# Left-over frequencies of the inverse feature transform stacked through HBM for tiles 6 to 15, and the sums of late tiles on GpSimd

## The chip, the cores and the metric

The kernel runs on one core of one Trainium2 chip. The metric is the device time of one execution in microseconds. Its engines are named as the profile names them: PE is TensorE, whose weight loads are PEld, DVE is VectorE, ACT is ScalarE, POOL is GpSimd, and SP is SyncE, which only issues transfers here. Each engine works through its own instructions in program order.

## What is computed

One block of a spectral network on 2048 tokens of 640 features, in float32: layer norm, a two-dimensional real Fourier transform over tokens and features, a filter, the inverse transform and a residual; then layer norm, a bilinear gated feed-forward of width 1728, and a residual.

```python
def _A_ref(x, w_r, w_i):
    X = rfft2(x, axes=(-2, -1))
    X = X * (w_r + 1j * w_i)
    return irfft2(X, s=(S, D), axes=(-2, -1))

def _B_ref(x, w_gate, w_up, w_down):
    h = einsum("bsd,df->bsf", x, w_gate) * einsum("bsd,df->bsf", x, w_up)
    return einsum("bsf,fd->bsd", h, w_down)

h = x + _A_ref(_layernorm(x), w_r, w_i)
h2 = h + _B_ref(_layernorm(h), w_gate, w_up, w_down)
```

## The kernel before, in words

The transform runs as products with tables of cosines and sines. Tokens are split in 16 tiles of 128 (`t`, 0 to 15). First comes the token transform of each tile (`s1_mm`), then, for 16 groups of token frequencies `g`, the feature transform (`d_mm`), the filter and the first half of the inverse token transform (`is2_mm`). Its result lies in `qm` (the 4 x 128 main feature frequencies, float32) and `qr` (64 left-over frequencies, 128 to 191, and frequency 192 in row 0; rows 0 to 63 hold the high part of each value, rows 64 to 127 the low part, both in float32r).

The stage that the change touches is the loop over `t` behind it. For each tile:

- `id_mm(t)`, the inverse feature transform, writes a pair of PSUM banks `eo`. Four float32 products of `qm` with the table `imt` (161 columns each; the profile counts each as two instructions) give even and odd halves of real and imaginary parts, and five float32r products of `qr` with the table `irt` (322 columns each) add the left-over frequencies. `irt` is part of the tile `xt`, whose second half is free until the transposes of tiles 4 to 7 write it.
- `unfold(t)`: ScalarE copies one half of `eo` to `s` (L650); VectorE forms sum and difference in `q` (L654, L655), then the first half of the output row, `yt` (L656); GpSimd forms the mirrored half (L658).
- `is1_mm(t)`, the last token transform, multiplies `yt` with the table `cit` into PSUM `y`; `acc(t)` (L671 with a running total for tiles 0 to 7, L669 for the rest) adds it to the residual `X[t]`.

The loop issues, for each `t`: the transposes of a normalised tile from `t` = 9 on (`turn_mm`, `y<-ident,zb` in the profile; `turn_hi` on ScalarE and `turn_lo`, L716, on VectorE), `unfold(t + 2)`, `id_mm(t + 3)`, side work on ScalarE (`aside`: squares for the layer norm L192, weight pieces L599, the normalisation L686), `is1_mm(t)`, `acc(t)`. `eo` has two pairs of banks, so `id_mm(t + 3)` waits until `unfold(t + 1)` has read its pair. The small scale operations of the layer norm (L188, L194, L202 to L205, L679, on 2 or 3 columns) are spread among VectorE's operations of `unfold` by `zipped`, which divides a list of side work evenly over the main operations.

The loads of three weight pieces (`raw0`) are issued on SP ahead of the loop. The next load on SP, `load_raw(0)` (L868), uses the space of `cit` and so waits for the last `is1_mm`. In the forward transform the same left-over work is stacked already for groups 5 to 14: `spread` writes rows of `s1r` to a scratch tensor in HBM (`sfar`), `stack` reads them back so that 99 rows hold high, low and high parts, and `d_mm` uses four passes for six.

```python
parts((ps[:, 0], ps[:, 1]), main,
      [(b, qr[:, k, t], irt[:, c]) for c, b, k in ((0, 0, 0), (2, 0, 0), (1, 1, 1), (3, 0, 1), (4, 1, 1))])
```

Of the kernel before, what the change touches and what calls it, by code (L numbers as in the profile page):

```python
# [25 lines left out]
RWHERE = ((1, 0), (0, 0), (1, 160), (0, 160))  # L26
RW = (160, 194, 162, 162)
PLAIN, LAST = 5, 15
AGAIN = {0: (5, 3), 1: (8, 2, "qt"), 5: (10, 3), 7: (13, 2, "qt")}
NR = 4  # L30
AHEAD = 5
# [8 lines left out]
def view(t, offset, dims):  # L40
    return bass.AP(tensor=t.tensor, offset=t.offset + offset, ap=[list(t.ap[0])] + [list(d) for d in dims])


def f32(ap):
    return ap.bitcast(F32)


def zipped(main, side):
    n = len(main)
    for i, f in enumerate(main):  # L50
        f()
        for h in side[i * len(side) // n:(i + 1) * len(side) // n]:
            h()
# [21 lines left out]
def tile_spectral_glu(ctx: ExitStack, tc: tile.TileContext, x, wf, wgu, wlast, wdown, wdlast,  # L75
                      cc, ci, fmain, frem, imain, irem, mm, out):
    nc = tc.nc
# [4 lines left out]
    far = ctx.enter_context(tc.tile_pool(name="far", bufs=1, space=bass.MemoryType.DRAM))  # L82
    ctx.enter_context(tc.manual_schedule())

    tt, act = nc.vector.tensor_tensor, nc.scalar.activation
# [28 lines left out]
    def mmx(o, l, r, start, stop):  # L114
        nc.tensor.matmul(o, l, r, start=start, stop=stop, skip_group_check=True)  # L115
# [13 lines left out]
    def home(tag, shape, name, dt=F32):  # L129
        return keep.tile(shape, dt, tag=tag, name=name)  # L130
# [142 lines left out]
    def s1_main(t, ps, a, b):  # L273
        act(view(s1, 4 * t + 2048 * a, [[2048, b - a], [64, 32], [1, 4]]),
            ps[:, a * P:b * P].rearrange("p (c g m) -> p c g m", c=b - a, g=32), AF.Copy)
# [18 lines left out]
    for ts, when, aside, root in GROUPS:  # L294
        k = len(when)
# [16 lines left out]
    for t in range(NT):  # L312
        if t == 1:
            nc.gpsimd.dma_start(frall, frem)
        if t >= 1:
# [18 lines left out]
            if t < AHEAD - 1:  # L334
                s1_rest(t - 1)
                main = lambda: s1_main(t - 1, PS1[t - 1][0], 0, 4)
# [55 lines left out]
    qr = home("qr", [P, 2, NT, P], "qr", F32R)  # L392
    PD, T, PU, Y, PI = {}, {}, {}, {}, {}

    def parts(ps, main, rest):
        for k, (b, o, w, l, r) in enumerate(main):
            mmx(ps[b][:, o:o + w], l, r, k < 2, False)
        for k, (b, l, r) in enumerate(rest):
            mmx(ps[b][:, 0:NQ], l, r, False, k >= len(rest) - 2)
# [21 lines left out]
    def stack(g, n, tag="dC"):  # L421
        o = home(tag, [P, 4, n, P], "st", F32R)
        src = sfar[:, :, :, g - PLAIN:g - PLAIN + n].rearrange("q l r g n -> q (l r) (g n)")
        for a, b, r in ((0, 66, 0), (66, 99, 0)):
            nc.sync.dma_start(f32(o[a:b].rearrange("p q g n -> p q (g n)")),
                              src[:, r:r + b - a].rearrange("q r n -> r q n"))
        for i in range(n):
            ST[g + i] = o[:, :, i]
# [9 lines left out]
    def s2_mm(g):  # L438
        if g >= NG - 2:
            ps = PU[g] = bank("re"), bank("im")  # L440
        else:
            PU[g] = pools["y"].tile([P, 2, 512], F32, tag="u", name="u", bufs=1)
            ps = PU[g][:, 0], PU[g][:, 1]
        for h in range(2):
            nc.tensor.matmul(ps[h][:, 0:NQ], WM[g][0][:, h], T[g][:, h], start=True, stop=True)  # L445
# [92 lines left out]
    for g in range(NG - 1):  # L538
        s2_mm(g)
        if g + 2 < NG:  # L540
            d_mm(g + 2)
        if g >= 5 and g in AGAIN:
            stack(*AGAIN[g])
        if g + 3 == NG:
            xt = home("big", [P, 2, 5, 2, 512], "xt", F32R)
            irt = xt[:, 1].rearrange("p k l n -> p (k l n)")[:, 0:5 * NQ].rearrange("p (c q) -> p c q", c=5)
        if g == NG - 2:
            nc.gpsimd.dma_start(irt, irem)
        if g == NG - 2:
            s2_mm(g + 1)  # L550
            filt_half(g, 0, True)
            is2_out(g - 2)
        if g >= 1:
            is2_mm(g - 1)
        if g < NG - 2:
            filt(g)
        else:
            late = [filt_half(g, 1), filt_half(g + 1, 0), filt_half(g + 1, 1, True)]
            for f in (late[0][0], late[1][0], late[1][1], late[2][1]):
                f()  # L560
        if g + 3 < NG:
            load_wm(g + 3)
        if g + 2 < NG:
            d_out(g + 2)
        if g >= 1:
            if g != NG - 3:
                is2_out(g - 1)
            if g + 2 < NG:
                load_wi(g + 2)
        if g < 2:  # L570
            stack(*AGAIN[g])
        elif g == 2:
            spread(PLAIN + 5, LAST)
        if g == 6:
            nc.sync.dma_start(cit, ci)
            nc.sync.dma_start(imt, imain)
# [26 lines left out]
    def load_direct(blk, raws, engine=nc.gpsimd):  # L603
        w = home("wA" if blk == 0 else "wB", [P, 3840], "wdir", F32R)
        return [split_in(NC - 1, cut(w, 0, 2, 640), wlast, raws[:1], engine),
                split_in(NC - 2, cut(w, 1280, 2, 1280), wgu[NC - 2], raws[1:], engine)]
# [29 lines left out]

    PE_, PY, YT, Z = {}, {}, {}, {}

    def id_mm(t):
        ps = PE_[t] = pair("eo")  # L640
        main = [(b, o, 161, qm[:, c, t], imt[:, c]) for c, (b, o) in enumerate(((0, 0), (1, 0), (0, 161), (1, 161)))]
        parts((ps[:, 0], ps[:, 1]), main,
              [(b, qr[:, k, t], irt[:, c]) for c, b, k in ((0, 0, 0), (2, 0, 0), (1, 1, 1), (3, 0, 1), (4, 1, 1))])

    def unfold(t, side, turns=()):
        ps = PE_[t]
        s = wk([P, 2, 161], "s")
        q = wk([P, 4, 161], "q")
        y = YT[t] = yt[:, t % 6]
        act(s, ps[:, :, 161:322], AF.Copy)  # L650
        for k in turns:
            turn_hi(k)
        zipped([
            lambda: tt(q[:, 0:2], ps[:, :, 0:161], s, op=OP.add),  # L654
            lambda: tt(q[:, 2:4], ps[:, :, 0:161], s, op=OP.subtract),  # L655
            lambda: tt(view(y, 0, [[320, 2], [1, 161]]), q[:, 0::2], q[:, 1::2], op=OP.add),  # L656
        ] + [lambda k=k: turn_lo(k) for k in turns], side)
        nc.gpsimd.tensor_tensor(view(y, 639, [[-320, 2], [-1, 159]]), q[:, 0::2, 1:160], q[:, 1::2, 1:160],  # L658
                                op=OP.subtract)

# [45 lines left out]
    def turn_hi(t):  # L706
        hi, pk = turned(t, 0)
        act(hi, pk, AF.Copy)
        if t == 0:
            TJ["b"] = home("dA", [P, 4, 4, P], "bt")  # L710
        if t < 4:
            act(TJ["b"][:, t], pk[:, 0:4], AF.Copy)

    def turn_lo(t):
        lo, pk = turned(t, 1)
        tt(lo, pk, f32(turned(t, 0)[0]), op=OP.subtract)  # L716
        if t % 8 >= 4:
            j = t % 4
            d = TJ[j] = wk([P, 4, P], "tj")
            b = TJ["b"][:, j]  # L720
            tt(d[:, 0:2], pk[:, 0:2], b[:, 0:2], op=OP.subtract)
            tt(d[:, 2:4], pk[:, 2:4], d[:, 0:2], op=OP.subtract)
# [62 lines left out]
    aside = [[] for _ in range(NT + 8)]  # L785
    dside = [[] for _ in range(NT + 8)]
    tside = [[] for _ in range(NT + 8)]
    scrap = xt[:, 1].rearrange("p k l n -> p (k l n)")[:, 2048:2048 + D]
    yt = home("wB", [P, 6, D], "yt")
    zb = home("dB", [P, 4, D], "zb")  # L790
    for ts in (range(3), range(3, 6), range(6, 8)):
        n, t0 = len(ts), ts[-1] + 1
# [11 lines left out]
    tside[NT - 1] = []  # L804
    raw0 = home("dA", [P, 3, D], "raw0")
    jobs = load_direct(0, [raw0[:, i] for i in range(3)])
    for i, (h, l) in enumerate((h, l) for hs, ls in jobs for h, l in zip(hs, ls)):
        aside[1 + i] += [h, l]
    id_mm(0)
# [274 lines left out]
    for n, (blk, p) in enumerate(steps):  # L1084
# [143 lines left out]
        for ci in range(2):  # L1228
            c = 2 * p + ci
            side = {n: [] for n in range(8)}  # L1230
# [41 lines left out]
            if blk == 0 and c in (6, 8):  # L1272
# [10 lines left out]
                for i in range(4):  # L1283
                    k = 4 * (c // 2 - 3) + i
# [10 lines left out]
def tables():  # L1295
# [19 lines left out]
    def rows(kind, ds):  # L1315
        r = np.zeros((len(ds), 2, NQ))
        for i, d in enumerate(ds):
# [3 lines left out]
            else:  # L1321
# [42 lines left out]
    def f4(a):  # L1364
        return np.ascontiguousarray(a, np.float32)

    def split(a):
        a = f4(a)
        hi = ((a.view(np.uint32) + np.uint32(0x800)) & np.uint32(0xFFFFF000)).view(np.float32)
        return f4(np.stack([hi, a - hi], 1))  # L1370

    inv = np.zeros((2, NF, 2, NQ))
    d = np.arange(161)
    for i, f in enumerate(fr):
        a = 1.0 if f in (0, 320) else 2.0
        o = slice(0, 161) if f % 2 == 0 else slice(161, 322)
# [54 lines left out]
```

## Time and profile before

| what | us |
|---|---|
| median of 3 runs | 687.5 (686.91 to 688.5) |
| profiled execution | 688.04 |
| its span, first to last instruction | 686.3 |
| granted TensorE clock over the span | 1.000 |
| the loop over tiles, first `eo` to the last load of weights behind it | 111.36 to 167.57 |
| VectorE's sums L656, 16 of them | 8.1 busy |
| GpSimd's sums L658, 16 of them | 16.2 busy |

The profiled execution is one run; its time is the span and what lies around it. A row of the timeline gives start and duration, engine, line, operation, output and inputs with their shapes. PE's matmuls overlap, so the step between two starts, not the duration, tells what one costs. "idle before" at a row's end is how long the engine stood still ahead of it, and what ended that.

### The profile page before, as it was taken

The numbers are of one execution on the slowest core, as the hardware profiler recorded it, in microseconds if no ns is written. First come the engines' busy times: TensorE is split into PE (matmuls) and PEld (weight loads), VectorE is DVE, ScalarE is ACT, GpSimd is POOL, SyncE is SP. The second block draws the span as 40 slices with busy tenths as digits, with TensorE's granted clock in tenths as the row PEclk, the third lists the DMA queues.
The fourth block names the chain that finished last, engine by engine and source line by source line (L and its number), as shares of the span: only waits on it lengthen the run. The fifth ranks groups of instructions, "written<-read, shape, count | busy, mean of one in ns | idle before, by whom it ended". The sixth has DMA issues, their size and how long they took to land.

```text
span 686.3 us, 10307 instructions
## 1 busy us (share of the span) xinstructions
PE 673.0 (98%) x3724; PEld 593.1 (86%) x3724; DVE 479.5 (70%) x975; ACT 322.0 (47%) x623; POOL 387.6 (56%) x367
## 2 busy tenths in 40 slices
PE   8999999999999999999999999999999999999998
PEld 8988888887888888888888889788888888888887
DVE  7968886788863968776766647753757575766654
ACT  6976665375533434263635236542525252525310
POOL 3101124521097887786887633286987878797610
PEclk9999999999999999999999999999999999999999
DMA  9749973001120212134243239200212121212003
GB/s 329 195 117 240 244 216 107 1 1 58 34 77 27 76 39 77 39 92 102 78 72 103 76 83 280 98 5 35 77 38 77 40 77 38 77 40 77 1 1 153
DMA packets 47299, 61.73 MB, mean 90 GB/s; under 512 B 24016, under 2 KB 30464, under 8 KB 47248
## 3 DMA queue, kind: packets, MB, share of 16 engines
q1 hardware_dynamic: 46528, 58.85, 28.9%
q0 software_dynamic: 288, 1.83, 0.7%
q8 instruction: 29, 0.48, 0.3%
q10 hardware_dynamic: 432, 0.39, 0.2%
q14 instruction: 22, 0.18, 0.1%
HBM read 51.84 MB, written 9.22 MB: 89 GB/s over the span
## 4 chain that ended last, share of the span: by engine, by line
PE 75%; DVE 11%; ACT 5%; issue 2%; POOL 2%; DMA 2%; SPq 1%; DVEq 0%; ACTq 0%
PE e L115 37%; PE d L115 24%; PE u L445 3%; PE re L115 2%; PE im L487 2%; PE eo L115 2%; PE im L115 2%; PE im L248 1%; PE y L115 1%; POOL wst L880 1%; SPq L1278 1%; PE ir L487 1%; DVE ht L985 1%; DVE fold L230 1%; ACT wst L891 1%
## 5 line engine op out<-in xcount | busy, mean ns | idle before, releaser
L115 PE MATMUL e<-xt,wst 128*128 128x512 f32 x864 | 213.4, 391 | 0.4 <-ACT c L1029 0.3
L115 PEld LDWEIGHTS e<-xt,wst 128*128 128x128 f32 x864 | 159.7, 188 | 31.5 <-ACT c L1029 0.9
L966 DVE TENSOR_TENSOR x<-d,x 128x320 f32<-128x320 f32 x280 | 123.4, 484 | 48.8 <-PE d L115 44.3
L115 PE MATMUL d<-wd,ht 128*128 128x320 f32 x832 | 143.0, 308 | 0.0
L115 PEld LDWEIGHTS d<-wd,ht 128*128 128x128 f32 x832 | 130.8, 188 | 7.3
L115 PE MATMUL e<-t,wst 128*128 128x512 f32 x360 | 94.5, 392 | 0.7 <-ACT h L1021 0.7
L880 POOL TENSOR_TENSOR wst<-raw,wst 128x1024 fp32r<-128x1024 f32 x23 | 56.4, 2453 | 64.8 <-ACT wst L879 49.0
L115 PEld LDWEIGHTS e<-t,wst 128*128 128x128 f32 x360 | 66.2, 188 | 14.1 <-ACT h L1021 1.5
L115 PE MATMUL d<-wt,ht 128*128 128x320 f32 x360 | 69.6, 311 | 0.5 <-DVE x L966 0.5
L896 POOL TENSOR_TENSOR wst<-raw,wst 128x896 fp32r<-128x896 f32 (+1 forms) x46 | 65.0, 1435 | 6.9 <-ACT wst L891 6.9
L115 PEld LDWEIGHTS d<-wt,ht 128*128 128x128 f32 x360 | 57.3, 188 | 3.4 <-issue 1.0
L1036 DVE TENSOR_TENSOR e<-e,h 128x512 f32<-128x512 f32 x24 | 16.8, 700 | 45.5 <-PE e L115 36.0
L891 ACT ACTIVATE wst<-raw 128x896 fp32r<-128x896 f32 (+1 forms) x48 | 30.2, 677 | 36.3 <-POOL raw L885 35.5
L1021 ACT ACTIVATE h<-e 128x512 f32<-128x512 f32 x24 | 14.3, 595 | 68.2 <-PE e L115 63.5
L982 ACT ACTIVATE ht<-e 128x512 fp32r<-128x512 f32 x44 | 26.2, 597 | 40.4 <-DVE e L1040 17.5
L115 PE MATMUL e<-xt,wdir 128*128 128x512 f32 x180 | 42.6, 394 | 1.1 <-DVE ht L834 1.1
L516 POOL CAST qr<-bits 1x128 fp32r<-1x128 f32 x15 | 4.2, 280 | 69.7 <-DVE qr L520 69.7
L115 PEld LDWEIGHTS e<-xt,wdir 128*128 128x128 f32 x180 | 33.4, 188 | 9.1 <-DVE ht L834 1.3
L985 DVE TENSOR_TENSOR ht<-e,ht 128x512 fp32r<-128x512 f32 x54 | 37.0, 685 | 1.6 <-ACT ht L982 1.3
L941 DVE TENSOR_TENSOR x<-d,x 128x320 f32<-128x320 f32 x62 | 27.5, 485 | 14.3 <-PE d L115 14.3
L620 ACT ACTIVATE wd<-draw 128x320 fp32r<-128x320 f32 (+1 forms) x30 | 15.7, 558 | 42.7 <-POOL draw L629 42.3
L600 POOL TENSOR_TENSOR wd<-draw,wd 128x640 fp32r<-128x640 f32 x8 | 12.4, 1573 | 39.3 <-ACT wd L599 39.3
(219 smaller groups left out, 1211.1 us busy)
## 6 DMA issues: line engine op xcount, KB each, us to landing
raw<-in_wgu_dram SPq DMA_DIRECT2D x24, 640.0 KB
draw<-in_wdown_dram SPq DMA_DIRECT2D x24, 320.0 KB
wts<-in_wf_dram SPq DMA_DIRECT2D x18, 322.0 KB
x<-in_x_dram SPq DMA_DIRECT2D x15, 320.5 KB
out_dram<-x SPq DMA_DIRECT2D x15, 320.0 KB
bits<-in_mm_dram SPq DMA_DIRECT2D x32, 128.0 KB
zfar<-zr SPq DMA_DIRECT2D x32, 80.0 KB
wts<-in_wf_dram SPq DMA_DIRECT2D x14, 161.0 KB
```

The source lines that it names most:

```text
L115: nc.tensor.matmul(o, l, r, start=start, stop=stop, skip_group_check=True)
L445: nc.tensor.matmul(ps[h][:, 0:NQ], WM[g][0][:, h], T[g][:, h], start=True, stop=True)
L487: nc.tensor.matmul(out, y[:, h, a:b], inv(g, h), start=n == 0, stop=n == len(ys) - 1)
L620: act(o[:, 0, a:a + n], src, AF.Copy)
L880: ptt(wa[:, 1], stage[:, 0:1024], f32(wa[:, 0]), op=OP.subtract)
L891: act(ws[:, 0, o:o + b - a], stage[:, a:b], AF.Copy)
L896: ptt(ws[:, 1, o:o + b - a], stage[:, a:b], f32(ws[:, 0, o:o + b - a]), op=OP.subtract)
L941: tt(xv, ps[b][:, 0:320], xv, op=OP.add)
L966: tt(xv, o, xv, op=OP.add)
L982: act(hop[:, a, 0], src, AF.Copy)
L985: engine.tensor_tensor(hop[:, a, 1], src, f32(hop[:, a, 0]), op=OP.subtract)
L1036: tt(ob, ob, h1, op=OP.add)
```

## The change

Tiles 6 to 15 take the left-over frequencies in four passes. `ispread` writes `qr` of these tiles to a scratch tensor `ifar` in HBM: by real and imaginary part, by half of the frequencies (33 rows each) and by high and low part. `istack` reads it back for tiles 6 to 9, 10 to 12 and 13 to 15 (`IPARTS`) into 99 rows: high and low parts, and the high parts again. Each of the four passes is 162 columns wide, because a left-over frequency belongs to one half of the output alone. Their table `sirt` holds high parts twice and low parts, and comes with `irem`, now 2258 columns for 1610. The stacks of tiles 6 to 9 and 13 to 15 lie in one place of `xt` (`near`), so the third waits for `id_mm(9)`; that of 10 to 12 lies in the space `dC`.

From tile 7 on, L656's sum goes to GpSimd (`near_sum`), ahead of the mirrored half. With one main operation fewer, `zipped` puts the side work elsewhere.

```diff
+IPLAIN = 6
+SUMS = 7
+IPARTS = ((6, 4), (10, 3), (13, 3))
...
-            irt = xt[:, 1].rearrange("p k l n -> p (k l n)")[:, 0:5 * NQ].rearrange("p (c q) -> p c q", c=5)
+            flat = xt[:, 1].rearrange("p k l n -> p (k l n)")
+            irt, sirt = cut(flat, 0, 5, NQ), cut(flat, 5 * NQ, 4, 162)
+            scrap, near = cut(flat, 2258, D), cut(flat, 2258 + D, 4, 4, P)
         if g == NG - 2:
-            nc.gpsimd.dma_start(irt, irem)
+            nc.gpsimd.dma_start(flat[:, 0:2258], irem)
...
+    SI = {}
+    ifar = far.tile([2, 2, 2, 33, NT - IPLAIN, P], F32, name="ifar")
+
+    def ispread():
+        for l in range(2):
+            for h in range(2):
+                r = 64 * l + 31 * h
+                nc.sync.dma_start(ifar[:, h, l, 1 - h:33].rearrange("b r t n -> r b t n"),
+                                  f32(qr[r:r + 32 + h, :, IPLAIN:NT]))
+        for b in range(2):
+            nc.sync.dma_start(ifar[b, 0, :, 0], f32(qr[0:65:64, 1, IPLAIN:NT]))
+
+    def istack(t, n):
+        o = near[:, :, 0:n] if t != 10 else home("dC", [P, 4, 3, P], "si", F32R)
+        src = ifar[:, :, :, :, t - IPLAIN:t - IPLAIN + n].rearrange("b h l r t n -> (l r) (b h) (t n)")
+        nc.sync.dma_start(f32(o[0:66]).rearrange("p q t n -> p q (t n)"), src)
+        nc.sync.dma_start(f32(o[66:99]).rearrange("p q t n -> p q (t n)"), src[0:33])
+        for i in range(n):
+            SI[t + i] = o[:, :, i]
...
+        if t not in SI:
+            parts((ps[:, 0], ps[:, 1]), main,
+                  [(b, qr[:, k, t], irt[:, c]) for c, b, k in ((0, 0, 0), (2, 0, 0), (1, 1, 1), (3, 0, 1), (4, 1, 1))])
+            return
+        parts((ps[:, 0], ps[:, 1]), main, [])
+        for q, (b, h) in enumerate(((0, 0), (0, 1), (1, 0), (1, 1))):
+            mmx(ps[:, b, 160 * h:160 * h + 162], SI[t][0:99, q], sirt[0:99, q], False, h == 1)
+        if t == 9:
+            istack(*IPARTS[2])
...
+        near_sum = lambda engine: engine.tensor_tensor(view(y, 0, [[320, 2], [1, 161]]), q[:, 0::2], q[:, 1::2],
+                                                       op=OP.add)
         zipped([
             lambda: tt(q[:, 0:2], ps[:, :, 0:161], s, op=OP.add),
             lambda: tt(q[:, 2:4], ps[:, :, 0:161], s, op=OP.subtract),
-            lambda: tt(view(y, 0, [[320, 2], [1, 161]]), q[:, 0::2], q[:, 1::2], op=OP.add),
-        ] + [lambda k=k: turn_lo(k) for k in turns], side)
+        ] + [lambda: near_sum(nc.vector)] * (t < SUMS) + [lambda k=k: turn_lo(k) for k in turns], side)
+        if t >= SUMS:
+            near_sum(nc.gpsimd)
...
     jobs = load_direct(0, [raw0[:, i] for i in range(3)])
+    ispread()
+    for t, n in IPARTS[:2]:
+        istack(t, n)
```

The row order on VectorE in `unfold(9)`, from the residual add of tile 6 (`x_74`) to that of tile 7, before:

```order
L671 SCALAR_TENSOR_TENSOR x_74,total<-y,x_74 128x640
L654 TENSOR_TENSOR q<-eo,s 128x322
L202 RECIPROCAL r<-sd 128x3
L655 TENSOR_TENSOR q<-eo,s 128x322
L203 SCALAR_TENSOR_TENSOR w<-r 128x3
L204 TENSOR_TENSOR w<-w,ve 128x3
L656 TENSOR_TENSOR yt<-q 128x2x161
L205 SCALAR_TENSOR_TENSOR r<-w,r 128x3
L679 SCALAR_TENSOR_TENSOR b<-m_1317,r 128x3
L671 SCALAR_TENSOR_TENSOR x_75,total<-y,x_75 128x640
```

The same place of VectorE in the changed kernel, whose line numbers are 3 and then 34 or 35 higher:

```order
L706 SCALAR_TENSOR_TENSOR x_74,total<-y,x_74 128x640
L688 TENSOR_TENSOR q<-eo,s 128x322
L205 RECIPROCAL r<-sd 128x3
L206 SCALAR_TENSOR_TENSOR w<-r 128x3
L689 TENSOR_TENSOR q<-eo,s 128x322
L207 TENSOR_TENSOR w<-w,ve 128x3
L208 SCALAR_TENSOR_TENSOR r<-w,r 128x3
L714 SCALAR_TENSOR_TENSOR b<-m_1318,r 128x3
L706 SCALAR_TENSOR_TENSOR x_75,total<-y,x_75 128x640
```

The sum into `yt` is gone from VectorE, and three scale operations follow one another behind the second write of `q`, which is also what releases GpSimd's two sums.

On SP's queue, from the loads of `raw0` to the first load behind the loop, before:

```order
L389 DMA bits<-in_mm_dram 128x256 x2
L598 DMA raw_1336<-in_wlast_dram 128x640
L598 DMA raw_1336<-in_wgu_dram 128x640 x2
L868 DMA raw<-in_wgu_dram 128x1280
L598 DMA draw<-in_wdlast_dram 128x640 x2
```

The same place of SP's queue in the changed kernel (`xt` is the place `near`):

```order
L603 DMA raw_1337<-in_wgu_dram 128x640 x2
L651 DMA ifar<-qr 32x2x1280
L651 DMA ifar<-qr 33x2x1280
L651 DMA ifar<-qr 32x2x1280
L651 DMA ifar<-qr 33x2x1280
L654 DMA ifar<-qr 2x1280 x2
L659 DMA xt<-ifar 66x4x512
L660 DMA xt<-ifar 33x4x512
L659 DMA si<-ifar 66x4x384
L660 DMA si<-ifar 33x4x384
L659 DMA xt<-ifar 66x4x384
L660 DMA xt<-ifar 33x4x384
```

Twelve transfers now stand between the loads of `raw0` and `load_raw(0)`: six out, and three pairs back.

More of the change, by code (lines that the diff above doesn't have):

```diff
@@ L641, in id_mm @@
         main = [(b, o, 161, qm[:, c, t], imt[:, c]) for c, (b, o) in enumerate(((0, 0), (1, 0), (0, 161), (1, 161)))]
-        parts((ps[:, 0], ps[:, 1]), main,
-              [(b, qr[:, k, t], irt[:, c]) for c, b, k in ((0, 0, 0), (2, 0, 0), (1, 1, 1), (3, 0, 1), (4, 1, 1))])
+        if t not in SI:
[7 more added lines that the diff above has]
+            istack(*IPARTS[2])
     def unfold(t, side, turns=()):
@@ L787, in tile_spectral_glu @@
     tside = [[] for _ in range(NT + 8)]
-    scrap = xt[:, 1].rearrange("p k l n -> p (k l n)")[:, 2048:2048 + D]
     yt = home("wB", [P, 6, D], "yt")
@@ L1387, in tables @@
     irem[0, 3] = irem[64, 3] = inv[0, 192, 0]
+    sirem = np.zeros((128, 4, 162), np.float32)
+    for q, (b, h) in enumerate(((0, 0), (0, 1), (1, 0), (1, 1))):
+        t = np.zeros((33, 162))
+        if h:
+            t[1:] = inv[b, 160:192, b, 160:322]
+        else:
+            t[1:] = inv[b, 128:160, b, 0:162]
+            t[0] = inv[b, 192, b, 0:162]
+        th, tl = split(t).transpose(1, 0, 2)
+        sirem[0:99, q] = np.concatenate([th, th, tl])
+    irem = np.concatenate([irem.reshape(128, -1), sirem.reshape(128, -1)], 1)
     stacked = np.zeros((128, sum(RW)), np.float32)
```

## The prediction, made before the changed kernel was timed

> **What bounds the kernel now.** I read the page's busy shares first, then the windows around the stage that the change touches (the inverse feature transform, from the first write of `eo` at 111.36 us to the last `is1_mm` at 167.5 us), then the chain of waits through it.
>
> ```profile
> PE 673.0 (98%) x3724; PEld 593.1 (86%) x3724; DVE 479.5 (70%) x975; ACT 322.0 (47%) x623; POOL 387.6 (56%) x367
> ...
> 111.36:131.79 20.43, 20.37 (x125) 18.45 (x125) 13.85 (x33) 7.39 (x18) 11.97 (x13) 1.00 0.00 1
> 131.79:144.23 12.44, 12.44 (x73) 10.90 (x74) 10.31 (x28) 5.78 (x14) 4.16 (x5) 1.00 0.00 1
> 144.23:161.00 16.77, 15.64 (x92) 12.75 (x92) 15.96 (x38) 13.09 (x26) 4.84 (x5) 1.00 0.00 1
> ```
>
> The columns of a window are its length, then busy time and instructions of PE, PEld, DVE, ACT and POOL, the granted clock, the DMA share and GB/s. Over the whole span PE is the bound. In this stage that holds up to 144 us (PE 12.44 of 12.44); behind it, where the transposes begin, VectorE is busy 15.96 of 16.77 us. GpSimd has room everywhere (4.84 of 16.77) and the DMA engines do nothing.
>
> The chain of waits says which engine is late at each place (start, duration, what):
>
> ```profile
> 111.36 7.63 PE eo L115 x52
> ...
> 128.11 0.64 DVE m L188
> ...
> 129.70 0.63 ACT wdir L599
> 130.33 0.32 ACT s L650
> ...
> 131.79 2.07 PE eo L115 x13
> ...
> 146.37 0.41 DVE q L655
> 146.80 0.04 DVE yt L656
> ...
> 147.21 0.82 DVE xt L716
> ...
> 150.18 0.71 DVE w L204
> ...
> 160.19 1.31 PE y L115 x4
> 161.50 3.45 PE e L115 x15
> ...
> 167.57 0.33 SPq L868
> ...
> 168.01 4.09 DMA draw<-in_wdlast_dram
> ```
>
> Early, PE follows PE. Before 131.79 the chain leaves it: L188 on VectorE, then ScalarE, whose in-order queue puts `s` of tile 6 (L650) late, and `id_mm(8)` at 131.79 waits for that tile's `eo` to be read. From 146 it runs over VectorE's L654, L655, L656, L716, L669. At 160.19 PE takes it back. The load issued at 167.57 waits for the last `is1_mm` (it reuses the space of `cit`), and the whole feed-forward part hangs on it. So what the stage gains by 167.5 us, the end gains.
>
> **The cut from five passes to four.** One tile on PE now, and the forward transform, which already uses four stacked passes:
>
> ```profile
> 119.90 1.26 PE L115 MATMUL eo<-tab,qm 128*128 128x161 f32 x8
> ...
> 120.89 1.01 PE L115 MATMUL eo<-xt,qr 128*128 128x322 f32 x5
> ...
> 121.75 1.24 PE L115 MATMUL y<-yt,tab 128*128 128x320 f32 x4
> ...
> 122.82 0.30 PE L115 MATMUL eo<-tab,qm 128*128 128x161 f32 x1
> ...
> 61.99 0.35 PE L115 MATMUL im<-frt,st 99*128 99x160 f32 x1
> 62.17 0.29 PE L115 MATMUL re<-frt,st 99*128 99x194 f32 x1
> 62.30 0.26 PE L115 MATMUL im<-frt,st 99*128 99x162 f32 x1
> 62.40 0.27 PE L115 MATMUL re<-frt,st 99*128 99x162 f32 x1
> 62.51 0.60 PE L487 MATMUL ir<-bits,y 128*65 128x128 f32 x4
> ```
>
> Matmuls overlap, so starts are subtracted. A tile is 0.99 (main) + 0.86 (five passes) + 1.07 (`is1_mm`) = 2.92 us. A 162-wide pass with 99 rows steps 0.10 to 0.11, the first behind the main group 0.18: four cost 0.18 + 3 x 0.105 = 0.50 us (0.42 if the first is no dearer, 0.52 by the row with the 194-wide pass). That saves 0.36 a tile, 3.6 over tiles 6 to 15; a tile becomes 2.56. Not all of it reaches the end:
>
> - Tiles 6 and 7 (0.72): nothing. `id_mm(8)` at 131.79 waits for the chain L188, L599, L650 above, which starts from work before tile 6. PE only idles longer.
> - Tiles 8, 9, 10, from 131.79 to `id_mm(11)`: PE-bound (VectorE is busy 10.31 of the 12.44 us there), so 3 x 0.36 = **1.1 us**.
>
> **The sum on GpSimd.** Prices, from the groups by form:
>
> ```profile
> L656 DVE TENSOR_TENSOR yt<-q 128x322 f32<-128x322 f32 x16 | 8.1, 504 | 0.4
> ...
> L470 POOL TENSOR_TENSOR us<-us,wts 128x322 f32<-128x322 f32 x2 | 1.7, 871 | 0.1
> ...
> L658 POOL TENSOR_TENSOR yt<-q 128x318 f32<-128x318 f32 x16 | 16.2, 1012 | 26.7 <-DVE q L655 11.0 <-DVE w L203 6.7 <-PE eo L115 6.4
> ```
>
> VectorE loses L656 in tiles 7 to 15, 9 x 0.50 = 4.5 us; GpSimd gains 9 of about 0.87, so near 1.8 us a tile with L658, in a period of 2.6 to 3.6. `yt` comes about 0.9 us later; nothing pays, since `is1_mm(t)` stands two tiles behind `unfold(t)`. If that cover were gone, each tile would pay up to 0.9.
>
> - Tile 11, up to `id_mm(12)` at 144.23: PE would save 0.36, but the first transpose needs L679 through ScalarE. I take **0.2** (0.4 if L679 is on time, -0.5 if it waits for GpSimd twice).
> - `id_mm(12)` at 144.23 to `y` of tile 13 at 160.19, 15.96 us, four tiles: VectorE's 15.96 busy lose 4 x 0.50; PE needs at least 4 x (0.60 transpose + 0.99 + 0.50 + 1.07) = 12.6, the 0.60 being the step from 148.09 to 148.69 between the transposes and `eo`. So between 0.6 (waits come back) and 3.3. I take 4 x 0.45 = **1.8**, near VectorE's end, as the chain goes through L656 in each of these tiles.
>
> The first transpose step:
>
> ```profile
> 148.09 0.77 PE L698 MATMUL y<-ident,zb 128*128 128x128 f32 x5 [0.66 <-DVE xt L716]
> ...
> 148.69 1.26 PE L115 MATMUL eo<-tab,qm 128*128 128x161 f32 x8
> ```
>
> From `y` of tile 13 on PE runs by itself, so nothing is added. The longer `irem` load (324 KB more, on GpSimd's queue) is needed only behind the main group of tile 0, at 111.36 + 0.99, and DMA stands at 0.00 from 111.36 on: nothing, or, if it were that tight, the 1.6 us that 324 KB take at 205 GB/s (below). **Sum: 1.1 + 0.2 + 1.8 = 3.1 us**, ends 1.2 and 4.8.
>
> **What is waited for anew.** VectorE's small operations already stand behind GpSimd:
>
> ```profile
> 140.37 0.16 DVE L204 TENSOR_TENSOR w<-w,ve 128x3 f32<-128x3 f32 x1
> ...
> 149.77 0.50 DVE L656 TENSOR_TENSOR yt<-q 128x322 f32<-128x322 f32 x1
> 149.90 0.97 POOL L658 TENSOR_TENSOR yt<-q 128x318 f32<-128x318 f32 x1 [2.00 <-DVE w L203]
> ...
> 150.18 0.71 DVE L204 TENSOR_TENSOR w<-w,ve 128x3 f32<-128x3 f32 x1
> ```
>
> The same L204 takes 0.16 ahead of GpSimd's operation and 0.71 beside it, ending with it (150.89 and 150.87). L656 started ahead and was not stretched. The change nearly doubles GpSimd's time, but also moves L188 up behind L655 in two tiles, where it can start before GpSimd does, so I take no net cost outside tile 11.
>
> [...]
>
> The new transfers go behind the last write of `qr`, on SP's queue:
>
> ```profile
> 112.34 0.28 DVE L517 TENSOR_TENSOR qr<-bits,qr 1x128 fp32r<-1x128 f32 x1
> ...
> 41.06 2.53 SPq L418 DMA_DIRECT2D sfar<-s1r  x4
> ...
> 41.00:42.00 1.00, 1.00 (x9) 1.00 (x9) 0.97 (x3) 0.96 (x3) 0.00 (x0) 1.00 0.10 38
> 42.00:43.00 1.00, 1.00 (x6) 0.72 (x6) 0.00 (x0) 0.95 (x3) 0.00 (x0) 1.00 0.66 205
> ...
> 62.00:63.00 1.00, 1.00 (x11) 1.00 (x11) 0.95 (x3) 0.23 (x1) 0.13 (x1) 1.00 0.99 371
> ```
>
> Out to HBM: four of 320 to 330 KB and two of 10, 1.35 MB. The like spread of the forward transform, issued at 41.06, moved 205 GB/s, with its first bytes some 0.9 us after issue (a share of 0.10 in that us, 0.66 in the next). So 112.6 + 0.9 + 6.6 = 120.1; the stack for tiles 6 to 9 (99 rows x 4 x 2 KB, 0.81 MB) 0.9 + 4.0 more: 125.0 us (120.2 at the 371 GB/s of the last row). It is wanted by the passes of tile 6, a tile after the row at 122.82 and behind its main group: 122.82 + 2.92 + 0.99 = 126.7; as PE waits for 131.79 anyway, lateness is free by the 0.72 of above, up to 127.4. Nothing else of SP's queue hurries: the next load there is that of 167.57. The third stack waits for `id_mm(9)` (about 136) and is wanted by `id_mm(13)` some ten us later.
>
> **The rivals.**
>
> *The HBM trip comes late* (the slower side). Past 127.4 each us of lateness is a us lost; the gain is gone at 130.5, and 0.2% slower (1.4 us, about what a measurement of this kernel tells from no change) at 131.9. That takes a rate under 2.16 MB in 17.5 us, 123 GB/s. At half of the 205 the data is there at 135.4, 8.0 late, and the time is 687.5 - 3.1 + 8.0 = 692.4. For it: the share of 0.66 shows that such transfers, from 32 or 33 partitions, don't fill the engines. Against: 205 was measured with just such ones, and DMA is idle now. Chance 0.09.
>
> *GpSimd gives the time back.* The scale operations of tile 9's `unfold` (L204, L205, L679 behind one another) may each wait for one GpSimd operation of 0.87, 2 x 0.87 less the 0.55 (0.71 - 0.16) that one pays now, 1.2 us, and the groups at tiles 12 and 14 0.35 more each, the rest of theirs lying beside L716. Loss 1.9, gain 1.2: 686.3. Against: at 140.37 L204 came first. Chance 0.17. [...]
>
> *PE sets the pace to the end*: if all waits beyond tile 8 vanish, 4.8 us, 682.7. For it: PE 12.6 against VectorE 14 in the last four tiles, close. Against: ScalarE's in-order queue stays. Chance 0.14.
>
> *Only the cut counts* (VectorE's freed time was cover, not path): 1.1 + 0.2, inside the second rival's bound; the VectorE rows of the chain speak against it, and I count it there.
>
> **The numbers.** Forecast, chance 0.60: 3.1 us less. The profiled execution took 688.04 us (span 686.3 and 1.7 around it), so it would take 684.9; the median of the runs, 687.5, is 0.5 lower, so 684.4. Faster by over 0.2%: 0.60 + 0.14 = 0.74; within: 0.17; slower: 0.09. The range takes in the PE-bound end and most of the second rival: 682.6 to 686.9.
>
> **What would show it.** Right: `eo<-xt` with four 162-wide passes in about 0.50 us; `id_mm(8)` still near 131.8 and `id_mm(12)` near 142.9; `y` of tile 13 near 157; the load after the last `is1_mm` near 164.5. Wrong: PE waiting on a DMA at tile 6 near 126.7, or at 10 or 13; L204, L205 or L679 at 0.8 us or more each; GpSimd's sums near 1.5 us instead of 0.87; `is1_mm` waiting for POOL.

## The result, and the profile after

The changed kernel takes 684.57 us (median of 4 runs, 684.45 to 685.28); the kernel before, run beside it, 688.0 us (median of 4, 686.91 to 688.85). The ratio is 0.9953, with a 95% interval from 0.9936 to 0.997: 3.2 us faster, between 2.1 and 4.4. The profiled run took 684.51 us, its span 682.7.

The page's busy shares of the changed kernel, and the three windows of the stage (same columns as before: length, then PE, PEld, DVE, ACT, POOL, granted clock, DMA share, GB/s):

```profile
PE 668.4 (98%) x3714; PEld 590.5 (86%) x3714; DVE 476.7 (70%) x966; ACT 321.9 (47%) x623; POOL 391.9 (57%) x376
...
111.36:131.79 20.43, 19.55 (x121) 17.84 (x122) 13.85 (x33) 7.40 (x18) 12.00 (x13) 1.00 0.52 137
131.79:144.23 12.44, 12.44 (x80) 11.02 (x78) 9.66 (x28) 7.15 (x17) 6.86 (x10) 1.00 0.18 50
144.23:161.00 16.77, 15.67 (x94) 12.81 (x92) 14.42 (x34) 11.92 (x23) 7.38 (x11) 1.00 0.00 1
```

VectorE fell from 15.96 to 14.42 us in the last window and GpSimd rose from 4.84 to 7.38. In the first window PE's busy time fell by 0.8 us, and ahead of the passes of tile 6 it waits 0.88 us. The chain of waits says for what (start, duration, what):

```profile
112.47 0.20 SPq L651
...
117.34 3.36 DMA ifar<-qr
120.84 0.29 SPq L659
121.19 6.53 DMA xt<-ifar
127.72 0.14 issue
127.86 0.65 PE eo L118 x4
...
148.82 0.62 DVE r L208
...
157.31 1.31 PE y L118 x4
158.62 3.45 PE e L118 x15
...
164.69 4.82 DMA raw<-in_wgu_dram
```

The trip through HBM is now on the chain: it lands at 127.72. `y` of tile 13 starts at 157.31 (160.19 before), the load behind the stage at 164.69 (167.57): the stage gained 2.88 us, 3.1 forecast. One tile on PE in the changed kernel's timeline:

```profile
132.08 1.26 PE L118 MATMUL eo<-tab,qm 128*128 128x161 f32 x8
133.07 0.69 PE L118 MATMUL eo<-xt 99*128 99x162 f32 x4
133.59 1.27 PE L118 MATMUL y<-yt,tab 128*128 128x320 f32 x4
134.71 1.26 PE L118 MATMUL eo<-tab,qm 128*128 128x161 f32 x8
```

Starts subtracted, it is 0.99 + 0.52 + 1.12 = 2.63 us, where the prediction had 2.56. GpSimd's two sums, by form (`x16` of L693 includes the tiles before 7):

```profile
L693 POOL TENSOR_TENSOR yt<-q 128x318 f32<-128x318 f32 x16 | 14.1, 882 | 6.5 <-DVE q L689 6.5
L685 POOL TENSOR_TENSOR yt<-q 128x322 f32<-128x322 f32 x9 | 6.8, 753 | 13.6 <-DVE q L689 6.3 <-DVE m L191 3.0 <-DVE w L206 2.9
```

The new sum takes 0.75 us, not 0.87, and the old one, 1.01 on average before, 0.75 wherever L685 has left VectorE (137.47, 140.30, 148.67 us). That sets up the questions: does each part give what its term in the sum said, what did the late trip cost, and do the sums on GpSimd cost anything.

### The profile page after: what moved, and what is told of

It is laid out like the page before. It is cut to its first block, busy times and chain, and to the rows that moved or that the text cites. A ratio compares the mean times of both kernels' runs of the same rounds, so it can differ in the third digit from the quotient of the medians.

```text
span 682.7 us, 10310 instructions
## 1 busy us (share of the span) xinstructions
PE 668.4 (98%) x3714; PEld 590.5 (86%) x3714; DVE 476.7 (70%) x966; ACT 321.9 (47%) x623; POOL 391.9 (57%) x376
## 4 chain that ended last, share of the span: by engine, by line
PE 79%; DVE 7%; DMA 5%; ACT 4%; POOL 3%; issue 1%; SPq 1%; ACTq 0%; POOLq 0%; DVEq 0%
PE e L118 39%; PE d L118 24%; PE u L448 3%; PE re L118 2%; DMA x<-in_x_dram 2%; PE im L118 2%; PE im L490 2%; PE y L118 2%; PE eo L118 2%; DMA raw<-in_wgu_dram 1%; PE im L251 1%; PE ir L490 1%; DMA xt<-ifar 1%; DVE ht L1022 1%; POOL wst L917 1%
```

## The experiments

**How they are compared.** Whole times scatter by more than these effects, and the place where the stage begins moves: the changed kernel starts `id_mm(0)` at 111.34 us in one profile and at 113.01 in another (e5), with the delay at 85 us, in the stage ahead. So each profile is read from its own `id_mm(0)`. The table's us are differences of starts in the timelines: `eo<-tab,qm` of tiles 0, 8 and 12, and `y<-yt,tab` of tile 13. The ratios, to the kernel before run beside each, stand in the last column.

| kernel | id0 to id8 | id8 to id12 | id12 to y13 | id0 to y13 | ratio (95%) |
|---|---|---|---|---|---|
| before | 20.43 | 12.44 | 15.96 | 48.83 | 1 |
| after | 20.74 | 11.04 | 14.19 | 45.97 | 0.9953 (0.9936 to 0.997) |
| e1 cut only | 20.95 | 12.08 | 15.93 | 48.96 | 0.9989 (0.9977 to 1.0) |
| e2 sums only | 20.43 | 12.27 | 14.60 | 47.30 | 0.9966 (0.9954 to 0.9978) |
| e3 tile 6 plain | 20.42 | 11.12 | 14.19 | 45.73 | 0.9945 (0.993 to 0.9959) |
| e4 no sum | 20.42 | 11.12 | 13.66 | 45.20 | 0.9933 (0.9907 to 0.9958) |
| e5 after again | 20.98 | 11.05 | 14.17 | 46.20 | 0.9958 (0.994 to 0.9977) |
| e6 spread twice | 29.81 | 11.05 | 14.16 | 55.02 | 1.0105 (1.0073 to 1.0137) |
| e7 tile 6 plain, sums from 5 | 19.90 | 11.05 | 14.20 | 45.15 | 0.9933 (0.9913 to 0.9952) |
| e8 as after, sums from 5 | 20.62 | 11.05 | 14.20 | 45.87 | 0.9951 (0.9934 to 0.9967) |
| e9 small transfers on ScalarE | 20.44 | 11.05 | 14.15 | 45.64 | 0.9945 (0.9927 to 0.9963) |
| e10 and second stack on GpSimd | 20.45 | 11.04 | 14.15 | 45.64 | 0.9945 (0.9925 to 0.9965) |
| e11 e7 again | 19.91 | 11.04 | 14.21 | 45.16 | 0.9946 (0.9927 to 0.9964) |
| e12 second stack on GpSimd | 20.55 | 11.04 | 14.21 | 45.80 | 0.9943 (0.9924 to 0.9962) |

**e1, the cut alone.**

```diff
-SUMS = 7
+SUMS = 16
```

> The change with the sum left on VectorE in all tiles (only the cut from five passes to four, with its trip through HBM). Theory A, the sum of the prediction, in which each part gives what its own term says: tiles 8 to 11 give about 1.1 (what after measured up to id_mm(12)), the tiles behind nothing, since VectorE, 15.96 us busy of 16.77, paces them: 1.1 less than before. Theory B, the two engines hold the pace in turn and each part needs the other: before id_mm(12) as in A less what L656 on VectorE takes back, 0.4 to 0.6 in all. Theory C, the cut is what counts and the sum was no matter: 2.9 us, as in after. Read from the stage itself: id_mm(12) to y of tile 13 is 15.96 before and 14.19 after; A and B say 15.6 to 16.0, C 14.2.

From `id_mm(8)` to `id_mm(12)` it gains 0.36 us of 12.44, behind that 0.03, and it gives the 0.52 us by which the trip is late at `id_mm(8)` (20.95) back: nothing is left at the end of the stage. The 0.39 lie just under B's 0.4 to 0.6, far from A's 1.1. The waits of PE from 130 us on, in e1 (waiting line, what for, us in total, times, longest):

```profile
PE y L733 <- DVE xt L751: 1.5, 4, 0.7
PE eo L118 <- DVE q L689: 0.4, 1, 0.4
...
PE eo L118 <- DVE w L206: 0.2, 1, 0.2
```

The passes that PE no longer does turn into waits for VectorE, 2.4 us in all, where before has 1.0 in the same window (0.7 for L716, 0.3 for L669). This holds also ahead of 144 us, where the prediction had called the stage PE-bound: tiles 8 and 9 do give 0.37 and 0.28 us, but `id_mm(11)` waits 0.23 and `id_mm(12)` 0.41, and 0.36 of the four tiles is left. What stands ahead of the first of these waits, in e1's timeline:

```profile
137.52 0.72 DVE L191 TENSOR_SCALAR m<-total 128x3 f32<-128x3 f32 x1
...
139.26 0.42 ACT L682 ACTIVATE s<-eo 128x322 f32<-128x322 f32 x1
...
140.88 1.34 PE L118 MATMUL eo<-tab,qm 128*128 128x161 f32 x8 [0.23 <-DVE w L206]
```

L191 takes 0.72 us beside GpSimd's sum (L693, 137.25 to 138.22) and ends with it; ScalarE, which waits for it (L195), comes late to `s` of tile 9, and `q` and then PE follow (the row names L206, the operation behind `q`). The edit that moves the sums also moves this L191 up, ahead of GpSimd's sum. In after it is

```profile
136.53 0.16 DVE L191 TENSOR_SCALAR m<-total 128x3 f32<-128x3 f32 x1
```

**e2, the sums alone.**

```diff
-    ispread()
-    for t, n in IPARTS[:2]:
-        istack(t, n)
```

> The change without its spread and stacks: five passes of 322 in every tile, as before, and the sums of tiles 7 to 15 on GpSimd (the longer irem load stays). Theory A, the sum of the prediction: the 1.8 us of tiles 12 to 15 all come, id_mm(12) to y of tile 13 about 14.2, and nothing before id_mm(12): 1.8 less than before. Theory B, both engines hold the pace: a transposing tile on PE is 0.60 + 0.99 + 0.86 + 1.07 = 3.52 us, VectorE's 15.96 less 4 x 0.50 is 13.96, 3.49 a tile, so with five passes PE takes over: 1.2 to 1.4 less than before, id_mm(12) to y of tile 13 14.6 to 14.8. Theory C, only the cut counts: no difference from before.

15.96 falls to 14.60, the 14.6 to 14.8 of B. All waits of PE from 118 to 165 us in e2:

```profile
PE y L118 <- DVE x L704: 0.5, 1, 0.5
```

One wait is left: the other tiles run at PE's pace with five passes, 3.46 us between transposes (144.97, 148.43, 151.89). In us of the stage behind `id_mm(8)`: the cut alone gives 0.39, the sums alone 1.53, both 3.17 (28.40 to 25.23). **1.25 us come only when both are there.** The ratios are too wide to show that by themselves. What counts here as the sums is the whole edit, with the small operations that it puts elsewhere (L191 takes 0.16 us in e2 too); no run has one without the other, so their shares stay open.

**e3, tile 6 with five passes.**

```diff
-IPLAIN = 6
+IPLAIN = 7
-IPARTS = ((6, 4), (10, 3), (13, 3))
+IPARTS = ((7, 3), (10, 3), (13, 3))
```

> The stacked passes from tile 7 on in place of tile 6, so that nothing is wanted from HBM before about 129.5 and the first stack is 0.6 MB and not 0.8. The theory that the late landing (127.7, id_mm(8) at 132.08 and not 131.79) cost 0.3 us: id_mm(8) at about 131.8 and the stage 0.3 us earlier than after, the time 684.3. The theory that it cost all that tiles 8 to 10 gave too little (0.65 of 1.1): 0.45 us, 684.1. Rival, tiles 6 and 7 shift nothing because the chain through ScalarE ends at 131.8 in either case, and what is late there is something else: no difference from after.

`id_mm(8)` comes 0.32 us earlier than in after, at the 20.42 of the kernel before, and the stage ends 0.24 earlier: the first theory. So the late trip cost 0.3 us and not all that was missing in tiles 8 to 10.

**e4, the sums of tiles 7 to 15 left out** (in these tiles the first 161 columns of `y`'s input are an earlier tile's).

```diff
-        if t >= SUMS:
-            near_sum(nc.gpsimd)
```

> The change with the sum of tiles 7 to 15 left out altogether (the first 161 columns of y's input stay as an earlier tile left them in those tiles): neither VectorE nor GpSimd does it. What the sums on GpSimd still cost the path. Theory A, nothing, as near L693 they lie beside other work: no difference from after (684.6), VectorE's small operations stretched as in after. [...] Bound of the PE: 4 x (0.60 + 0.99 + 0.52 + 1.12) = 12.9.

Of the 14.19 us from `id_mm(12)` to `y` of tile 13 0.53 go, so A falls: the sums on GpSimd cost the path something. L208 is stretched at two places, in tiles 12 and 14. First after, then e4 (timeline; e4's lines behind the sum are two lower):

```profile
148.74 0.69 DVE L208 SCALAR_TENSOR_TENSOR r<-w,r 128x3 f32<-128x3 f32 x1
...
152.91 0.77 PE L733 MATMUL y<-ident,zb 128*128 128x128 f32 x5 [0.64 <-DVE xt L751]
...
155.67 0.52 DVE L208 SCALAR_TENSOR_TENSOR r<-w,r 128x2 f32<-128x2 f32 x1
```

```profile
148.52 0.15 DVE L208 SCALAR_TENSOR_TENSOR r<-w,r 128x3 f32<-128x3 f32 x1
...
152.14 0.77 PE L731 MATMUL y<-ident,zb 128*128 128x128 f32 x5
...
154.91 0.15 DVE L208 SCALAR_TENSOR_TENSOR r<-w,r 128x2 f32<-128x2 f32 x1
```

0.54 + 0.37 us of stall go, but only the first is on the path: from `id_mm(14)` to `id_mm(15)` after takes 4.03 us and e4 3.48, as PE's wait for L751 is gone, and from there to `y` of tile 13 they take 3.80 and 3.79. At both places L208 started behind a GpSimd sum and ended with it: in tile 12 0.07 us behind L693 (148.67 to 149.41, L208 to 149.43), in tile 14 0.25 behind (155.42 to 156.17, L208 to 156.19). In tile 9 it starts 0.03 us ahead of L685 (139.56, 0.16) and L714 stalls in its place in both kernels, 0.61 behind L685 in after and 0.64 behind the mirrored sum in e4, each to the end of that sum (140.36 for 140.35, 140.15 for 140.13). The traces show the stretch; what makes the operations wait they don't.

**e5, the changed kernel again.**

> The changed kernel unaltered, on the chip of the next three: a base for them, and a second look at where its gain comes from. The stage (id_mm(8) to y of tile 13 25.23 us, the load behind it issued at 164.69) should repeat within 0.2 us. Theory A, the 0.9 us that the first profile gained behind the stage (its feed-forward starts 2.5 us early at 190, and 3.8 early at 450) come from the change: the second block starts at 445 to 446 again, against 449.75 before. Theory B, that is how the loads of that execution happened to land: it starts anywhere from 444 to 448, while the stage's own shift of 2.5 to 2.9 us repeats.

From `id_mm(8)` on the stage repeats (25.22, 25.23). The trip was later, 16.76 us behind `id_mm(0)` and not 16.52. Behind the stage: after's load at 164.69 was 2.88 us early against before, its load at 429.29 3.80. That extra comes between the loads of 414 and 429 us: 15.10 us in after, 16.53 before, 15.00 in e5. In the other kernels, whose code is the same there, it is 14.38 to 15.93, and 14.79 and 14.38 in the two profiles of e7's kernel. It varies, as B says; but no profile except the one of before has 16.53, and whether before always has it stays open. It would fit that the ratios of e1 and e2 (0.8 and 2.3 us of 688) lie lower by some 0.8 us than their stages (0.13 longer, 1.53 shorter).

**e6, the spread sent twice,** first to a scratch that nobody reads.

```diff
-    ispread()
+    ispread(spare)
+    ispread(ifar)
```

> The change with the spread to HBM issued twice, first into a scratch of its own that nobody reads, so that the stacks come later by about the spread's own 6.6 to 8.5 us. Theory A, the rival of the prediction on record: each us of lateness behind the free point is a us lost, so the passes of tile 6 start at 134.5 to 136.4 (127.86 in after), id_mm(8) shifts by the same 6.6 to 8.5 and the time is 691 to 693. Theory B, a part is made up again behind tile 8, as VectorE, ScalarE and GpSimd work ahead while PE waits and the tiles behind are not bound by PE alone: id_mm(8) to y of tile 13 falls under 25.2, to 23.5 to 24.5, and the time is 690.

The time is 1.05% longer than before (0.73 to 1.37%), more than either theory said. PE in e6's timeline, then windows of e6 (columns as above):

```profile
127.44 1.26 PE L118 MATMUL eo<-tab,qm 128*128 128x161 f32 x8
136.12 1.11 PE L118 MATMUL eo<-xt 99*128 99x162 f32 x4 [7.41 <-DMA xt<-ifar]
137.03 2.41 PE L118 MATMUL y<-yt,tab 128*128 128x320 f32 x4
139.24 2.28 PE L118 MATMUL eo<-tab,qm 128*128 128x161 f32 x8
```

```profile
128.00:129.00 1.00, 0.70 (x6) 0.46 (x4) 1.00 (x4) 0.00 (x0) 1.00 (x1) 1.00 0.04 15
...
131.00:132.00 1.00, 0.00 (x0) 0.00 (x0) 0.00 (x0) 1.00 (x3) 0.00 (x0) 0.54 0.62 190
...
137.00:138.00 1.00, 1.00 (x4) 0.78 (x4) 0.00 (x0) 0.67 (x2) 0.00 (x0) 0.50 0.72 186
...
141.00:142.00 1.00, 1.00 (x8) 1.00 (x7) 0.62 (x2) 0.03 (x1) 0.71 (x1) 0.84 0.00 0
```

The data is 6.53 us later than in after (23.05 against 16.52 us behind `id_mm(0)`), but `id_mm(8)` 9.07: while PE idled, its granted clock fell to 0.50, and the two tiles behind took 6.76 us (136.12 to 142.88) where after has 4.22. Nothing is made up later (25.21 against 25.23). Lateness of this size cost **more than a us for a us**, 9.07 for 6.53.

**e7, e3 with the sums on GpSimd from tile 5.** To e3's edit comes

```diff
-SUMS = 7
+SUMS = 5
```

> The stacked passes from tile 7 on (as in e3) and the sums on GpSimd from tile 5 on and not 7. Theory A: id_mm(8) waits for L191 of the second group, which stands behind L685 of tile 5 on VectorE and then 0.7 us behind L693 on GpSimd, and through L195 and L604 holds s of tile 6; with L685 of tile 5 gone from VectorE it runs 0.5 to 1.1 us earlier, s of tile 6 follows eo of tile 6, and id_mm(8) starts when PE is free, at about 131.4 (131.89 in e3): 0.5 us earlier than e3 to the end of the stage. Theory B, ScalarE's queue (L195 twice, L604) still ends at the same time as it is in order and full: id_mm(8) at 131.8, no difference from e3. Theory C, GpSimd, which has L605's 1.55 us there too, is late with the sums and y waits for it: later than e3.

Theory A: `id_mm(8)` at 131.27, 0.52 us earlier than e3 behind `id_mm(0)`. First e3's timeline, then e7's:

```profile
128.13 0.72 DVE L191 TENSOR_SCALAR m<-total 128x3 f32<-128x3 f32 x1
...
130.33 0.42 ACT L682 ACTIVATE s<-eo 128x322 f32<-128x322 f32 x1
...
131.89 1.34 PE L118 MATMUL eo<-tab,qm 128*128 128x161 f32 x8 [0.35 <-ACT s L682]
```

```profile
127.49 0.16 DVE L191 TENSOR_SCALAR m<-total 128x3 f32<-128x3 f32 x1
...
129.14 0.42 ACT L682 ACTIVATE s<-eo 128x322 f32<-128x322 f32 x1
...
131.27 1.26 PE L118 MATMUL eo<-tab,qm 128*128 128x161 f32 x8
```

L191 starts 0.64 us earlier and isn't stretched, `s` of tile 6 follows 1.19 earlier (0.10 of either is the earlier start of the stage, 111.37 for 111.47), and PE no longer waits there: the chain that held `id_mm(8)` in the prediction hung on a VectorE operation behind GpSimd. This is the best stage of all, 3.7 us under before and 0.8 under after, and e11 repeats it:

> The kernel of e7 again beside e9 and e10, to compare them on one chip: id_mm(8) 19.9 us behind id_mm(0), the stage as in e7 (id_mm(0) to y of tile 13 45.15 us, within 0.15), the time 0.5 to 1.1 below after's share of before: a ratio of 0.993 to 0.9945.

45.16 us again. The ratios of the two, 0.9933 and 0.9946, lie below after's 0.9953 and 0.9958, but the intervals overlap: over after the gain is shown in the stage, not by the whole time.

**e8 to e10 and e12: why the trip was late.** e8 moves the code of the second stack into `id_mm(5)` and takes the sums from tile 5:

```diff
+        if t == 5:
+            istack(*IPARTS[1])
```

> The stacked passes from tile 6 on, the second stack (tiles 10 to 12) issued only behind id_mm(5), so that the first has the DMA engines to itself, and the sums on GpSimd from tile 5 on. Theory A, the two stacks shared the rate: the first lands at 125.5 to 126.5 instead of 127.7, tile 6's passes start at 126.7 to 126.9 without a wait; together with L191's earlier start id_mm(8) comes at 131.0 (132.08 in after), and the stage ends 1.0 us earlier than in after. Theory B, the rate was that of the 0.8 MB stack by itself (about 190 GB/s whatever runs beside it): it lands at 127 or later, tile 6 waits as before, id_mm(8) at 131.5 to 132.

The edit doesn't do what was meant: SP's queue holds nothing else, so the stack was still issued right behind the first, at 121.76. What e8 then shows is the sums from tile 5 with the trip nearly unchanged: `id_mm(8)` comes 20.62 us behind `id_mm(0)` (20.74 in after), and the 0.12 is the trip's, as tile 6's passes start 16.40 us behind it (16.52). While the trip is late, L191's earlier start is worth nothing from `id_mm(8)` on.

e9 sends the two small transfers from ScalarE's queue:

```diff
-            nc.sync.dma_start(ifar[b, 0, :, 0], f32(qr[0:65:64, 1, IPLAIN:NT]))
+            nc.scalar.dma_start(ifar[b, 0, :, 0], f32(qr[0:65:64, 1, IPLAIN:NT]))
```

> As e8 (stacked passes from tile 6 on, sums on GpSimd from tile 5 on; there the second stack was still issued right behind the first, since nothing held SP's queue, so it was not later at all), with the two transfers of 10 KB of the spread issued by ScalarE's queue beside SP's. What made the trip land 2.7 us behind the 125.0 of the prediction. Theory A, the tail: after moves the spread's bulk until 119.3 but issues the first stack only at 120.84, as SP issues the two small ones behind the others (2.54 us) and waits for them; so with these beside the others the first stack is issued at 119.0 to 119.7, tile 6's passes start at 126.7 (no or 0.2 us of wait for the DMA) and id_mm(8) at 130.9 to 131.1, 1.1 us earlier than after and 0.2 to 0.4 earlier than e7. Theory B, the rate: the bulk takes until 119.3, a transfer out needs another 1.4 us until it is seen to be done whatever its size, and the stack is issued at 120.5 or later: id_mm(8) at 131.7 to 132.0 as in e8 (132.07), no gain.

The timeline of e9:

```profile
112.85 1.55 ACTq L654 DMA_DIRECT2D ifar<-qr  x2
114.45 0.44 ACT L682 ACTIVATE s<-eo 128x322 f32<-128x322 f32 x1 [2.33 <-DMA ifar<-qr]
120.82 0.29 SPq L659 DMA_DIRECT2D xt<-ifar  x1
```

B: with the small ones out of the way by 114.4 the stack is still issued at 120.82. And `s` of tile 0 stood behind them on ScalarE, so `id_mm(2)` came 0.8 us late (115.96, 115.14 in e7) and hid what the stack did. e10 adds the second stack on GpSimd's queue:

```diff
+        if t == 5:
+            istack(*IPARTS[1], nc.gpsimd)
```

> As e9, and the second stack (tiles 10 to 12) on GpSimd's queue behind q of tile 5, so that it starts at about 127.5 and not at 121.6. Theory A, the two stacks share the rate: the first has 190 GB/s for its 0.81 MB alone, 4.2 us instead of 5.5, and lands 1.3 us earlier than in e9, before it is wanted at 126.8; id_mm(8) at 130.9 to 131.0, and the second, landing at about 133, is wanted at 138. Theory B, the first stack had the rate to itself already, as the queue works in order: no difference from e9 in when it lands, and the time is e9's, or up to 0.5 later by the issue on GpSimd.

No wait for the trip, and none in e9 either, as tile 6 was late by itself: it doesn't tell the theories apart. e12 is e10 with the small transfers back on SP:

> As e10, but with the two small transfers back on SP's queue: in e9 and e10 they sat in front of s of tile 0 on ScalarE (2.33 us of wait) and id_mm(2) came 0.8 us late, which hid what the first stack did. Theory A, the two stacks share the rate, and the first alone lands at about 126.4 (in e10 the traffic of that stack ends in the us from 126 to 127): tile 6's passes start at 126.7 to 126.9 without a wait, id_mm(8) 19.6 to 19.7 us behind id_mm(0) (20.74 in after, 19.90 in e7), id_mm(0) to y of tile 13 44.8 to 44.9 (45.97 and 45.15), the shortest of all. Theory B, the stack lands at 127.5 or later also alone: tile 6's passes wait as in after, id_mm(8) 20.5 to 20.7 behind id_mm(0). Rival to both, GpSimd's 1.5 us of issuing at 128 makes its sums of tiles 5 and 6 late and y waits for it: id_mm(8) between 20.0 and 20.5 with PE waiting for POOL.

A falls. From its issue to the start of tile 6's passes the first stack takes 6.83 us alone on the DMA engines, and with the second behind it 6.66 (e4), 6.88 (e8), 7.01 (e1) and 7.02 (after and e5): no cost of sharing shows. Issue, traffic and start in e12:

```profile
122.57 0.30 SPq L659 DMA_DIRECT2D xt<-ifar  x1
...
127.00:128.00 1.00, 1.00 (x8) 0.84 (x7) 0.35 (x1) 0.06 (x1) 1.00 (x2) 1.00 0.72 190
...
128.20:128.70 0.50, 0.50 (x4) 0.26 (x2) 0.50 (x3) 0.00 (x0) 0.50 (x1) 1.00 0.15 33
128.70:129.30 0.60, 0.01 (x1) 0.00 (x0) 0.60 (x3) 0.00 (x0) 0.60 (x2) 1.00 0.00 0
...
129.40 0.65 PE L118 MATMUL eo<-xt 99*128 99x162 f32 x4 [0.69 <-DMA xt<-ifar]
```

The traffic thins from 190 to 33 GB/s and ends at 128.7, 6.1 us behind the issue, and the passes start 0.7 us later. The way out ends in the same manner in after:

```profile
118.00:119.00 1.00, 1.00 (x8) 0.99 (x7) 0.96 (x3) 0.00 (x0) 0.33 (x1) 1.00 0.67 205
...
119.40:120.20 0.80, 0.80 (x6) 0.64 (x5) 0.12 (x1) 0.66 (x2) 0.33 (x1) 1.00 0.10 38
120.20:120.80 0.60, 0.60 (x6) 0.60 (x6) 0.60 (x1) 0.00 (x0) 0.00 (x0) 1.00 0.00 0
```

Here it thins to 38 GB/s and ends at 120.2, and the stack behind it is issued at 120.84, 0.6 us later. So B's 1.4 us behind the bulk is for the most part the last pieces of the transfer itself, and 0.6 us lie behind its last byte. The two waits behind the last byte here, both on SP's queue, are 0.6 and 0.7 us; no run shows what fills them.

## Why the prediction held, step by step

- **The forecast** was 684.4 us in 682.6 to 686.9, and 684.57 came. The sum of the stage was 3.1 us, and 2.88 came. It is not right term by term, and that the whole time fits to 0.2 us is partly luck: the forecast starts from 687.5, and the kernel before, run beside the change, took 688.0.
- **The cut, 0.36 a tile.** Four passes step 0.52 us and not 0.50, and a tile saves about 0.3. The mechanism was right, the size nearly so.
- **Tiles 6 and 7, nothing.** They gave nothing, and less: the trip landed late and `id_mm(8)` moved by 0.3 us the wrong way.
- **Tiles 8 to 10, "PE-bound", 1.1; tile 11, 0.2.** From `id_mm(8)` to `id_mm(12)` 1.40 us came, 1.3 forecast, but as 0.94 and 0.46: two errors that cancel by luck. The step's reason holds for tiles 8 and 9 alone (e1: 0.37 and 0.28). In tiles 10 and 11 the cut by itself ends in waits for VectorE, and 0.36 of the four tiles is left. VectorE's 10.31 us of 12.44 were read as room; what binds in e1 is not that share but the order, a small operation beside GpSimd's sum, then ScalarE, then `s`. Only with the edit of the sums does PE's saving arrive in all four tiles.
- **Tiles 12 to 15, 1.8 from the sums.** 1.77 came. The sums alone gave 1.36 (e2), then PE with five passes held the pace. The prediction charged the whole to VectorE's account.
- **The trip, 125.0, with lateness free up to 127.4.** This step failed: it landed at 127.7, and the first of the named signs of being wrong, PE waiting on a DMA at tile 6, came. The way out was sized well, its last byte at 120.2 for 120.1. The sum left out what lies behind the last byte, 0.6 us out and 0.7 back. And the stack takes 6.1 us from issue to last byte (e12), where rate and first bytes gave 4.9: it starts slowly (31 and 115 GB/s in the us from 121 and from 122 in after, issued at 120.84) and its end is thin (33 GB/s, e12). The cost stayed at 0.3 us (e3), since the free point lay close. It lay at 127.57: in after 4.22 us pass from tile 6's passes to `id_mm(8)`, which came at 131.79 before. The prediction's 127.4 left out the 0.22 us that PE stood idle there already (128.65 + 2.92 = 131.57).
- **The rival of a late trip, a us for a us.** Just past the free point it holds (127.86 for 127.57, and 0.3 us lost). At 6.5 us more, e6 shows the price too low by 2.5 us, through the clock (0.50 over most of the two tiles behind).
- **The rival of GpSimd giving time back.** The waits it named are there (L208 0.69 and 0.52 us, 0.15 without the sum) and cost 0.53 us (e4), not 1.9, and at one of the places it named, tile 12. The stall in tile 14 lies beside PE's own time, and the one in tile 9 is there without the new sum too. GpSimd's own sums were shorter than priced (0.75 for 0.87).
- **The rival that only the cut counts** falls: the cut alone gives 0.39 us behind `id_mm(8)` (e1).
- **PE to the end, 682.7.** Not reached; PE still waits 0.64 us for L751 in tile 14 and 0.46 for L704.
- **Behind the stage** the 2.88 us arrive as 2.49 at 190 us (187.52 for 190.01), for the most part since the transfer waited for landed 4.82 us behind the load's issue (164.69 to 169.51) and not 4.53 (167.57 to 172.10). The profile's further gain past 414 us varies from run to run (e5) and is not put down to the change.

## What to carry to other kernels

In this stage behind `id_mm(8)`, where PE and VectorE are both over 80% busy (before: 12.44 and 10.31 us of 12.44, then 15.64 and 15.96 of 16.77), taking work from PE alone gave 0.39 us, the edit on VectorE alone 1.53, and both 3.17: price two such cuts together, and test each alone before crediting it. The busy share (10.31 of 12.44) did not tell the room here; the order of what one tile waits for did. The trip through HBM cost more than its bytes at the rate of a full us: a slow start (31 GB/s in the us from 121), a thin end (33 to 38 GB/s), and 0.6 to 0.7 us behind the last byte at each hop; add that before judging whether such a trip lands in time. And look for small VectorE operations behind a GpSimd sum on the chain: moving the sums of tiles 5 and 6 (e7) was worth more here, 0.58 us, than taking the wait for the trip away (e3), 0.24.

## What was not expected of the hardware

- After about 2.4 us without a matmul PE's granted clock halved, and it came back about 5.2 us after the matmuls resumed (e6). The last matmul ahead of the gap ended at 128.70, and the mean clock is 1.00 in the us from 130, 0.54 in that from 131 and 0.50 from 132 on, so it fell, by estimate, at about 131.08. The matmuls resumed at 136.12, and the mean clock is 0.50 up to 141, 0.84 in the us from there and 1.00 from 142, so it came back at about 141.3. In after, where PE stood idle for 0.88 us ahead of tile 6's passes, it stayed at 1.00. This is one gap in one profile; what sets the two delays is not shown.
- GpSimd's sum of 128x318 took 0.99 us on average from 131 to 161 us before, where VectorE did the tile's other sum beside it, and 0.78 in the same window after, where GpSimd did both, one behind the other: GpSimd's sum was stretched beside VectorE's as L208 was beside GpSimd's (0.69 us in after, 0.15 in e4 without the sum), and taking the new sum cost it less than the sum's own 0.75.
- Two transfers of 10 KB held SP's queue for 2.54 us (1.00 and 1.50), the four of 320 to 330 KB for 3.90.
